# Turning the attention's exponents in 32x32 blocks on VectorE instead of TensorE, from the 12th unit on

## The chip, the cores and the metric

The kernel runs on one core of a Trainium2 chip. The metric is device time in microseconds (us). The kernel before took 911.37 us (median of three runs, 910.83 to 912.17).

## What is computed

A windowed attention over 8 sequences of 576 tokens with 8 heads of 64, whose output feeds a two-layer network with a gate of its own. All of it is in float32.

```python
scores = scale * np.matmul(q, k.transpose(0, 1, 3, 2))          # B, H, S, D = 8, 8, 576, 64
mask_plain = (rel >= 0) & (rel < 32)                            # heads 0-3
mask_dil = (rel >= 0) & (rel < 32 * 4) & (rel % 4 == 0)         # heads 4-7
attn = np.exp(scores - np.max(scores, axis=-1, keepdims=True))
attn = attn / (np.sum(attn, axis=-1, keepdims=True) + 1e-09)
x = np.matmul(attn, v)            # then tokens x 512
h = x @ w_in                      # 4608 x 2048
g = h * erf(softplus(h))
out = g @ w_out                   # 4608 x 512
```

## The kernel before

**Units.** The attention is cut into 72 units of 256 queries for two heads. Dilated heads are reordered on the host, so every strip of 32 queries needs 64 keys. A unit has 8 strips. Its scores lie on 128 partitions (four strips `r` of 32 queries) in two parts `p`, each 64 keys wide, for two heads `h`: 128 x 256 numbers. A unit passes through these steps:

- `scores(n)`, TensorE: 32 matmuls of 32x64 results into the two banks `sp0`, `sp1` (line 221).
- `mask_max(n)`, VectorE: mask and row maximum, four groups of 128x64 (line 232).
- `exponents(n)`, ScalarE: exp and row sums (line 242).
- `normalize(u)`: reciprocal on VectorE (line 254), product on GpSimd (POOL, line 255).
- Three units later, `transposes(u)`, TensorE: two 128x128 transposes against an identity into PSUM (line 260), then `turned(u)`, VectorE: one copy of 128x256 to the tile `pT` (line 264). Now keys lie on partitions.
- `values(u)`, TensorE: 32 matmuls with 64 keys on 64 partitions, with `v` as the weights (line 279).
- `rows(u)`, ScalarE: copies the result out of PSUM (line 321).

**The network.** It works on 512 tokens at a time, in 72 steps `t` of two halves `j`. The loop over `x = 2t + j` gives each engine its work of one half step, in a fixed order written by hand. TensorE's order in one `x` is: the first product (`mm1`, line 528; from the fourth chunk `mm1_fast`, line 649), the second product of two steps earlier (`mm2`, line 702, 12 matmuls of 512 columns), then, if a unit is due, `values` and `scores` (`attend`). VectorE takes the first product out of its single PSUM buffer `h` (and `tx`): `take`, line 670, `take_fast`, lines 658 to 663. It then computes the gate (lines 684 to 688) and, while the weights are being split in two parts, `prep_dve` (lines 460 to 466). ScalarE does softplus and erf (lines 674, 677).

**Visits.** `visits()` tells in which `x` units are scored, and the same `x` turns and multiplies the units scored three units before. The first 14 units (`first_visit`) run before the loop; there units 0 to 10 are turned. Units 11 to 17 are turned singly in `x` = 0 to 6, units 18, 19, 20 singly in `x` = 9, 11, 14, units 21 to 70 in pairs in 25 visits from `x` = 19 to 99, and unit 71 in `x` = 103. For `x` below 4 the turn stands ahead of `mm1`; later it stands between `mm1` and `mm2`:

```python
if t < 2:
    turn(ready)
    weights(x)
...                       # mm1, take
if t >= 2:
    turn(ready)
```

All engines work through their instructions in order. Transfers are issued on one queue (SP), also in order, so a transfer that waits holds up those behind it.

Of the kernel before, what the change touches and what calls it, by code (L numbers as in the profile page):

```python
# [10 lines left out]
F32 = mybir.dt.float32  # L11
# [7 lines left out]
P = 128  # L19
# [45 lines left out]

FREE = FIRST - LAG + 4

EARLY = 2, 3, 4, 6, 7, 9, 10, 12, 13


# [37 lines left out]
def kind(n):  # L108

    it, strip = divmod(n, NSTRIP)  # L110
    at = strip * STRIP
    if it % HP >= HP // 2:

        e = (at + STRIP - 1) // RES * RES - at
        return 1 + EDGES.index(e) if e > -WIN else 0
    return 1 if strip == 0 else 0


def kinds(u, p):

    n = SPU * u + SIDE * p
    return tuple(kind(n + i) for i in range(SIDE))


PARTS = SPU // SIDE
# [4 lines left out]
def key_start(u, s):  # L130

    return s * STRIP + (WIN if (SPU * u) // NSTRIP != (SPU * u + s) // NSTRIP else 0)
# [7 lines left out]
def attn_moe_kernel(ctx: ExitStack, tc: tile.TileContext, qk, v, masks, eye, w_in, w_out, out):  # L140
# [31 lines left out]
        return qkz[u % 3 if u < DEEP else u % 2]  # L172

    vz = [one.tile([P, SIDE, 2, D], F32, name=f"v{i}") for i in range(2)]
    pz = [one.tile([P, n], F32, name=f"pT{i}") for i, n in enumerate((2 * P, TOK))]

    spb = [ps.tile([P, TOK], F32, name=f"sp{i}") for i in range(2)]
    sps = [b[:, 0:2 * PARTS * KEYS].rearrange("p (i b k) -> p i b k", i=2, k=KEYS) for b in spb]
# [35 lines left out]

    def scores(u):
        i, z = u % 2, qk_of(u)
        for s in range(SPU):
            at, (p, r) = QW + key_start(u, s), divmod(s, SIDE)
            for h in range(2):
                hs = slice(h * D, (h + 1) * D)  # L220
                nc.tensor.matmul(sps[h][r * STRIP:(r + 1) * STRIP, i, p, :], z[hs, s * STRIP:(s + 1) * STRIP],  # L221
                                 z[hs, at:at + KEYS], start=True, stop=True,
                                 tile_position=(h * D, r * STRIP))
# [37 lines left out]
                                in_=pr[:, PARTS * h:PARTS * (h + 1), :].rearrange("p a k -> p (a k)"), identity=ident)  # L261

    def turned(u, copy):
        copy(out=pz[u in second][:, 0:2 * P], in_=turn_place(u))

    def turn(units):
        for u in units:
            transposes(u)
        for u in units:
            turned(u, nc.vector.tensor_copy)  # L270

    def values(u):
        vt, pt = vz[u % 2], pz[u in second]
        for s in range(SIDE):
            qs = slice(s * STRIP, (s + 1) * STRIP)
            for p in range(PARTS):
                ks, xp = slice(p * KEYS, (p + 1) * KEYS), place(u, p)
                for h in range(2):
                    nc.tensor.matmul(xp[h * D:(h + 1) * D, qs], vt[ks, s, h, :],  # L279
                                     pt[ks, h * P + s * STRIP:h * P + (s + 1) * STRIP], start=True, stop=True,  # L280
                                     tile_position=(p * KEYS, h * D))
# [432 lines left out]
    def save():  # L714

        o = doubles(2).bitcast(F32).rearrange("p n w -> p (n w)")
        spare = small.tile([P, DM], F32, name="o", bufs=1)
        for tt in range(TOK // P):
            part = [o[:, 0:DM], o[:, DM:2 * DM], spare, pz[1]][tt]
            copy_for(tt)(out=part, in_=acc[tt])  # L720
            nc.sync.dma_start(out=partial[tt], in_=part)

# [21 lines left out]
    with tc.manual_schedule():  # L744
# [26 lines left out]
        for x in range(2 * (NT + 2)):  # L771
# [2 lines left out]
            scored, ready = [n for n in ns if has(n)], [n - LAG for n in ns]  # L774
            second.update(ready[1:])

            if t < 2:
                turn(ready)
                weights(x)
            if t < NT:  # L780
                after = STEPS[t + 1][0] if ends(t) and t + 1 < NT else None
# [22 lines left out]
                table(t - 1)  # L804
            if t < 2:
                attend(ready, scored)
            if t >= 2:
                turn(ready)

            while scaled:  # L810
                normalize(scaled.pop(0))
            scaled, fresh = fresh, []
# [74 lines left out]
def _values(a):  # L887

    p = _padded(a)
    w = np.stack([p[..., i * STRIP:i * STRIP + KEYS, :] for i in range(NSTRIP)], axis=2)  # L890
    w = w.reshape(NU, PARTS, SIDE, 2, KEYS, D).transpose(0, 1, 4, 2, 3, 5)
    return np.ascontiguousarray(w).reshape(NU, PARTS * KEYS, SPU * D)


def _masks():
# [38 lines left out]
```

## Time and profile before

| what | value |
|---|---|
| median of three runs | 911.37 us (910.83 to 912.17) |
| span of the profiled execution, first to last instruction | 908.9 us |
| mean granted TensorE clock | 0.994 |
| TensorE busy | 884.3 us, 97% |
| VectorE busy | 669.6 us, 74% |
| ScalarE busy | 600.7 us, 66% |
| GpSimd busy | 77.9 us, 9% |
| first half step `x` = 0 starts near | 50 us |
| last unit's `values` | 683 us |

The record holds the span of the profiled execution alone; the time outside the span was not recorded with it. The median of the timed runs lies 2.5 us above the span, and sums against the span are carried over to the median by this constant. In the rows of the profile a time is in microseconds from the start of the span; PE is TensorE, DVE VectorE, ACT ScalarE, POOL GpSimd, SPq the queue of transfers; an arrow in brackets names what ended the idle time ahead of an instruction.

### The profile page before, as it was taken

How to read it: one execution, taken by the hardware profiler on the slowest of the kernel's cores; microseconds unless marked ns; L12 is line 12 of the kernel's file. 1: busy time of each engine (PE TensorE's matmuls, PEld its weight loads, DVE VectorE, ACT ScalarE, POOL GpSimd, SP SyncE). 2: the span in 40 equal slices, each digit the busy share in tenths (PEclk: the TensorE clock that was granted, in tenths of full speed). 3: DMA queues.
4: the chain of work that ended last, by engine and by line, in shares of the span. 5: the costliest groups of instructions: out<-in, count | busy, mean ns of one | idle time of the engine just before them, and what ended most of it. 6: DMA issues, size and time to landing. Idle time of an engine off the chain costs nothing.

```text
span 908.9 us, 22857 instructions
## 1 busy us (share of the span) xinstructions
PE 884.3 (97%) x9129; PEld 753.5 (83%) x9129; DVE 669.6 (74%) x1702; ACT 600.7 (66%) x1267; POOL 77.9 (9%) x97
## 2 busy tenths in 40 slices
PE   7789999999999999999999999999999999999998
PEld 3367777888887888889989988888988999999996
DVE  3889879886688888668776777678666866776555
ACT  5889879876678687666776676669654644545442
POOL 2322100000011100000100000000000000000000
PEclk7999999999999999999999999999999999999999
DMA  8784444432458688687668765877567546655521
GB/s 276 250 273 149 137 159 135 136 127 80 150 199 324 232 284 309 241 284 227 219 206 283 262 213 191 289 266 252 185 237 230 185 146 230 233 180 203 199 84 47
DMA packets 69450, 188.89 MB, mean 208 GB/s; under 512 B 9184, under 2 KB 17632, under 8 KB 63200
## 3 DMA queue, kind: packets, MB, share of 16 engines
q1 hardware_dynamic: 69056, 186.91, 60.9%
q8 instruction: 72, 1.18, 0.5%
q10 hardware_dynamic: 288, 0.52, 0.1%
q14 instruction: 34, 0.28, 0.1%
HBM read 153.85 MB, written 33.55 MB: 206 GB/s over the span
## 4 chain that ended last, share of the span: by engine, by line
PE 85%; DVE 7%; DMA 3%; ACT 2%; issue 1%; POOL 1%; SPq 0%; DVEq 0%; POOLq 0%; ACTq 0%
PE acc L702 40%; PE h L649 15%; PE tx L649 12%; PE h L528 10%; PE sp L279 3%; PE sp L221 3%; PE sp L260 1%; DMA dbl<-in_w_in_dram 1%; DMA v<-in_v_dram 1%; DVE s L684 1%; DVE hc L670 1%; DVE w L465 1%; ACT prob L242 1%; DVE prob L232 1%; POOL prob L255 0%
## 5 line engine op out<-in xcount | busy, mean ns | idle before, releaser
L702 PE MATMUL acc<-wout_hi,ghi 128*128 128x512 f32 x576 | 228.4, 397 | 0.5 <-DVE ghi L687 0.4
L702 PE MATMUL acc<-wout_lo,ghi 128*128 128x512 f32 x576 | 225.7, 392 | 0.0
L674 ACT ACTIVATE s<-hc 128x1024 f32<-128x1024 f32 x72 | 76.5, 1062 | 189.4 <-DVE hc L663 171.2
L702 PE MATMUL acc<-wout_hi,glo 128*128 128x512 f32 x576 | 159.0, 389 | 0.0
L702 PEld LDWEIGHTS acc<-wout_hi,glo 128*128 128x128 f32 x576 | 108.1, 188 | 22.7
L702 PEld LDWEIGHTS acc<-wout_hi,ghi 128*128 128x128 f32 x576 | 108.6, 188 | 20.7 <-DVE ghi L687 0.9
L702 PEld LDWEIGHTS acc<-wout_lo,ghi 128*128 128x128 f32 x576 | 108.7, 189 | 19.5
L255 POOL TENSOR_TENSOR prob<-prob,rinv 128x256 f32<-128x256 f32 x72 | 69.0, 968 | 539.0 <-DVE ssum L253 314.1
L688 DVE TENSOR_TENSOR glo<-s,ghi 128x512 fp32r<-128x512 f32 x144 | 100.1, 695 | 5.5 <-PE acc L702 0.5
L242 ACT ACTIVATE prob<-prob,nmax 128x64 f32<-128x64 f32 x288 | 96.4, 338 | 7.6 <-DVE nmax L232 7.1
L684 DVE TENSOR_TENSOR s<-hc,s 128x1024 f32<-128x1024 f32 x72 | 92.9, 1290 | 9.2 <-ACT s L677 9.1
L528 PE MATMUL h<-x,win 128*128 128x512 f32 x384 | 96.6, 394 | 2.6 <-DVE hc L670 2.5
L649 PE MATMUL h<-win 128*128 128x256 f32 x720 | 98.1, 283 | 0.0
L674 ACT ACT_TABLE_LOAD x72 | 92.4, 1283 | 1.3
L677 ACT ACT_TABLE_LOAD x72 | 92.4, 1283 | 1.3
L649 PEld LDWEIGHTS h<-win 128*128 128x128 f32 x720 | 91.6, 192 | 0.0
L528 PEld LDWEIGHTS h<-x,win 128*128 128x128 f32 x384 | 71.2, 188 | 18.8 <-DVE hc L670 3.7
L677 ACT ACTIVATE s<-s 128x1024 f32<-128x1024 f32 x72 | 76.3, 1060 | 0.8
L232 DVE CUSTOM_DVE_ANT_0 prob<-sp,cst 128x64 f32<-128x64 f32 x288 | 45.4, 220 | 36.9 <-ACT rows L321 20.1
L687 DVE CAST ghi<-s 128x512 fp32r<-128x512 f32 x144 | 68.5, 475 | 3.1 <-PE acc L702 0.6
L321 ACT COPY rows<-sp 128x128 f32<-128x128 f32 (+7 forms) x167 | 27.9, 308 | 57.3 <-PE sp L221 55.0
L659 DVE TENSOR_TENSOR hc<-h,hc 128x512 f32<-128x512 f32 x48 | 33.2, 692 | 41.1 <-PE h L649 40.8
(110 smaller groups left out, 1257.6 us busy)
## 6 DMA issues: line engine op xcount, KB each, us to landing
win<-ws SPq DMA_DIRECT2D x48, 1024.0 KB, 5.5
win<-ws SPq DMA_DIRECT2D x48, 768.0 KB, 4.5
v<-in_v_dram SPq DMA_DIRECT2D x72, 256.0 KB, 4.1
qk<-in_qk_dram SPq DMA_DIRECT2D x45, 272.0 KB, 3.9
dbl<-in_w_in_dram SPq DMA_DIRECT2D x16, 512.0 KB, 4.0
dbl<-in_w_out_dram SPq DMA_DIRECT2D x16, 512.0 KB, 3.7
ws<-x SPq DMA_DIRECT2D x32, 256.0 KB, 4.1
xT<-rows SPq DMA_DIRECT2D x24, 288.0 KB, 5.0
```

What stands on the lines that cost most here:

```text
L232: nc.vector.tensor_tensor_reduce(out=pr[:, g, :], in0=sps[h][:, u % 2, p, :], in1=mask[QUADS.index(kinds(u, p))], scale=-SCALE, scalar=BIG ...
L242: nc.scalar.activation(out=probs[u][:, j, :], in_=probs[u][:, j, :], func=AF.Exp, scale=-1.0, bias=nmax[:, j:j + 1], accum_out=sums[u][:, ...
L255: nc.gpsimd.tensor_tensor(probs[u], probs[u], rinv.broadcast_to([P, 2 * PARTS, KEYS]), op=ALU.mult)
L528: nc.tensor.matmul(h, win_at[:, ftp, j, cc // 2, w, cc % 2, :], x[cc], start=(k == 0 and i == 0), stop=(k == CC - 1 and i == 2))
L649: nc.tensor.matmul((h, bank)[b][:, half * HN:(half + 1) * HN], w[:, k, wi, c, :], x[:, xi, c, :], start=(c == 0 and n == 0), stop=(c == 1 ...
L659: nc.vector.tensor_tensor(out=a[:, 0:2], in0=x, in1=a[:, 2:3].broadcast_to([P, 2, HN]), op=ALU.add)
L674: nc.scalar.activation(out=ls[t], in_=hs[t], func=AF.Softplus)
L677: nc.scalar.activation(out=ls[t], in_=ls[t], func=AF.Erf)
L684: nc.vector.tensor_tensor(out=e, in0=hc, in1=e, op=ALU.mult)
L687: nc.vector.tensor_copy(out=ghi, in_=e[:, j])
L688: nc.vector.tensor_tensor(out=glo, in0=e[:, j], in1=ghi.bitcast(F32), op=ALU.subtract)
L702: nc.tensor.matmul(acc[tt], g[:, tt * P:(tt + 1) * P], w[:, ft, :], start=(first and w is wout_hi and g is ghi), stop=(last and g is glo))
```

## The change

From unit 11 (`TURNED = FIRST - LAG`) on, TensorE no longer turns the exponents. VectorE does it from SBUF to SBUF, with an instruction that transposes 32x32 blocks, each within its 32 partitions. One instruction turns the whole 128x256 unit. Half of the blocks are then where `values` can use them; the other half must lie on the neighbouring 32 partitions, and four more instructions of 32 partitions x 128 elements turn these again and write them there. So that 64 keys come to lie on 64 neighbouring partitions, the strips of a unit are dealt to the partitions in another order (`strip_of`), the values and masks are laid out anew on the host, and the masks grow from 10 to 14 groups of 64 columns. `flip` stands at the head of `x`, ahead of `mm1` and `take`, for all later units. `pT` is one tile for both units of a pair, and `save` uses the tile `plain` in place of two others.

```diff
+TURNED = FIRST - LAG
...
 def kinds(u, p):
-    n = SPU * u + SIDE * p
-    return tuple(kind(n + i) for i in range(SIDE))
+    return tuple(kind(SPU * u + strip_of(u, p, r)) for r in range(SIDE))
+
+def strip_of(u, p, r):
+    return SIDE * p + r if u < TURNED else SIDE * (r // 2) + 2 * p + r % 2
...
     def turned(u, copy):
-        copy(out=pz[u in second][:, 0:2 * P], in_=turn_place(u))
-
-    def turn(units):
-        for u in units:
-            transposes(u)
-        for u in units:
-            turned(u, nc.vector.tensor_copy)
+        copy(out=pz[:, 0:2 * P], in_=turn_place(u))
+
+    def flip(units):
+        for i, u in enumerate(units):
+            to = pz[:, i * 2 * P:(i + 1) * 2 * P].rearrange("p (e g q) -> p e g q", e=2, q=STRIP)
+            src = probs.pop(u).rearrange("p g (e k) -> p e g k", e=2)
+            nc.vector.transpose(out=to.rearrange("p e g q -> p g e q"), in_=src.rearrange("p e g k -> p g e k"))
+            for r in range(SIDE):
+                y, q = r % 2, r ^ 1
+                nc.vector.transpose(out=to[q * STRIP:(q + 1) * STRIP, y], in_=src[r * STRIP:(r + 1) * STRIP, 1 - y])
...
     def values(u):
-        vt, pt = vz[u % 2], pz[u in second]
+        if u >= TURNED:
+            vt, at = vz[u % 2].rearrange("p (y a) h d -> p y a h d", y=2), (u in second) * 2 * P
+            for y in range(2):
+                for p in range(PARTS):
+                    for x in range(2):
+                        ks = slice(x * KEYS, (x + 1) * KEYS)
+                        qs = slice((2 * p + y) * STRIP, (2 * p + y + 1) * STRIP)
+                        for h in range(2):
+                            c = at + y * P + (PARTS * h + p) * STRIP
+                            nc.tensor.matmul(place(u, x)[h * D:(h + 1) * D, qs], vt[ks, y, p, h, :],
+                                             pz[ks, c:c + STRIP], start=True, stop=True,
+                                             tile_position=(x * KEYS, h * D))
+            return
...
     def save():
-        spare = small.tile([P, DM], F32, name="o", bufs=1)
-            part = [o[:, 0:DM], o[:, DM:2 * DM], spare, pz[1]][tt]
+            part = [o[:, 0:DM], o[:, DM:2 * DM], plain[:, TOK:2 * TOK], plain[:, 0:TOK]][tt]
...
+            flip(ready)
             if t < 2:
-                turn(ready)
                 weights(x)
...
-            if t >= 2:
-                turn(ready)
```

VectorE in `x` = 1, where unit 12 is turned: the masks of unit 14 end, then the turn, the weights, a remainder of the attention's result and `take`. Before:

```order
L232 ISA nmax 128x1
L264 COPY pT_88<-acc_94 128x256
L460 TENSOR_TENSOR win<-w,win 128x4x128
L464 TENSOR_SCALAR w<-w 128x512
L465 SCALAR_TENSOR_TENSOR w<-dbl_891,w 128x512
L466 SCALAR_TENSOR_TENSOR w<-dbl_891,w 128x512
L332 TENSOR_TENSOR wout_lo<-rows,wout_hi 128x448
L670 COPY hc<-h 128x512
```

After the change, in the same place:

```order
L239 ISA nmax 128x1
L278 STREAM_TRANSPOSE pT<-prob 128x4x2x32
L281 STREAM_TRANSPOSE pT<-prob 32x128 x4
L484 TENSOR_TENSOR win<-w,win 128x4x128
L488 TENSOR_SCALAR w<-w 128x512
L489 SCALAR_TENSOR_TENSOR w<-dbl_890,w 128x512
L490 SCALAR_TENSOR_TENSOR w<-dbl_890,w 128x512
L356 TENSOR_TENSOR wout_lo<-rows,wout_hi 128x448
L694 COPY hc<-h 128x512
```

Five instructions stand where one copy stood; nothing else moved here.

VectorE in `x` = 59, a visit of a pair (units 45 and 46). `w` at line 615 belongs to the next chunk, lines 662 and 663 are `take_fast`, 684 to 688 the gate. Before:

```order
L615 TENSOR_TENSOR w<-dbl_5166,x_97 128x512
L615 TENSOR_TENSOR w<-dbl_5167,dbl_5166 128x512
L662 TENSOR_TENSOR hc<-tx,hc 128x2x256
L663 TENSOR_TENSOR hc<-h,hc 128x512
L264 COPY pT_88<-sp_90 128x256
L264 COPY pT_89<-sp_91 128x256
L684 TENSOR_TENSOR s<-hc,s 128x1024
L687 CAST ghi<-s 128x512
L688 TENSOR_TENSOR glo<-s,ghi 128x512
```

After the change:

```order
L639 TENSOR_TENSOR w<-dbl_5232,x_96 128x512
L639 TENSOR_TENSOR w<-dbl_5233,dbl_5232 128x512
L278 STREAM_TRANSPOSE pT<-prob 128x4x2x32
L281 STREAM_TRANSPOSE pT<-prob 32x128 x4
L278 STREAM_TRANSPOSE pT<-prob 128x4x2x32
L281 STREAM_TRANSPOSE pT<-prob 32x128 x4
L686 TENSOR_TENSOR hc<-tx,hc 128x2x256
L687 TENSOR_TENSOR hc<-h,hc 128x512
L708 TENSOR_TENSOR s<-hc,s 128x1024
L711 CAST ghi<-s 128x512
L712 TENSOR_TENSOR glo<-s,ghi 128x512
```

The turn has moved from behind `take_fast` to ahead of it, and has ten instructions in place of two.

TensorE in the same visit, between `mm1_fast` and `mm2`, before:

```order
L649 MATMUL h<-win 128x256 x12
L260 MATMUL sp_90<-ident,prob 128x128 x2
L260 MATMUL sp_91<-ident,prob 128x128 x2
L702 MATMUL acc_93<-wout_hi,ghi 128x512
L702 MATMUL acc_93<-wout_lo,ghi 128x512
```

After the change the two rows of line 260 are gone and `mm2` follows `mm1_fast` at once; the rest of TensorE's list is the same, matmul by matmul, and so are ScalarE's, POOL's and the queue of transfers, but for the names of tiles and the wider transfer of the masks.

More of the change, by code (lines that the diff above doesn't have):

```diff
@@ L174, in attn_moe_kernel @@
     vz = [one.tile([P, SIDE, 2, D], F32, name=f"v{i}") for i in range(2)]
-    pz = [one.tile([P, n], F32, name=f"pT{i}") for i, n in enumerate((2 * P, TOK))]
+    pz = one.tile([P, TOK], F32, name="pT")
     spb = [ps.tile([P, TOK], F32, name=f"sp{i}") for i in range(2)]
@@ L216, in scores @@
         i, z = u % 2, qk_of(u)
-        for s in range(SPU):
-            at, (p, r) = QW + key_start(u, s), divmod(s, SIDE)
+        for p, r in np.ndindex(PARTS, SIDE):
+            s = strip_of(u, p, r)
+            at = QW + key_start(u, s)
             for h in range(2):
@@ L263, in turned @@
     def turned(u, copy):
-        copy(out=pz[u in second][:, 0:2 * P], in_=turn_place(u))
-    def turn(units):
-        for u in units:
-            transposes(u)
-        for u in units:
-            turned(u, nc.vector.tensor_copy)
-    def values(u):
-        vt, pt = vz[u % 2], pz[u in second]
+        copy(out=pz[:, 0:2 * P], in_=turn_place(u))
[7 more added lines that the diff above has]
+                nc.vector.transpose(out=to[q * STRIP:(q + 1) * STRIP, y], in_=src[r * STRIP:(r + 1) * STRIP, 1 - y])
+    def values(u):
+        if u >= TURNED:
[11 more added lines that the diff above has]
+            return
+        vt, pt = vz[u % 2], pz
         for s in range(SIDE):
@@ L890, in _values @@
     w = np.stack([p[..., i * STRIP:i * STRIP + KEYS, :] for i in range(NSTRIP)], axis=2)
-    w = w.reshape(NU, PARTS, SIDE, 2, KEYS, D).transpose(0, 1, 4, 2, 3, 5)
-    return np.ascontiguousarray(w).reshape(NU, PARTS * KEYS, SPU * D)
+    w = w.reshape(NU, SPU, 2, KEYS, D)
+    units = []
+    for u in range(NU):
+        if u < TURNED:
+            units.append(w[u].reshape(PARTS, SIDE, 2, KEYS, D).transpose(0, 3, 1, 2, 4))
+        else:
+            units.append(w[u].reshape(2, PARTS, 2, 2, KEYS, D).transpose(0, 4, 2, 1, 3, 5))
+    return np.stack([x.reshape(PARTS * KEYS, SPU * D) for x in units])
 def _masks():
```

## The prediction, made before the kernel was run

> **What bounds the kernel now.** I read the page first (busy shares), then the busy times by stage, then the two engines' timelines at the turns, then the waits. The profiled execution's span is 908.9 us; the median of the runs lies 2.5 us higher, and I add that at the end.
>
> ```profile
> span 908.9 us, 22857 instructions
> PE 884.3 (97%) x9129; PEld 753.5 (83%) x9129; DVE 669.6 (74%) x1702; ACT 600.7 (66%) x1267; POOL 77.9 (9%) x97
> ```
>
> TensorE is the bound on the average, and VectorE has a quarter of the span free. The average hides the stages:
>
> ```profile
> 54.00:75.00 21.00, 17.22 (x277) 12.85 (x255) 18.94 (x66) 18.93 (x46) 4.01 (x7) 1.00 0.82 278
> 75.00:97.00 22.00, 22.00 (x276) 17.29 (x275) 18.06 (x57) 19.69 (x57) 2.61 (x4) 1.00 0.44 136
> 97.00:143.00 46.00, 44.31 (x371) 34.98 (x370) 39.80 (x85) 36.53 (x67) 5.93 (x5) 1.00 0.41 133
> 143.00:245.00 102.00, 102.00 (x919) 84.05 (x921) 78.25 (x186) 76.63 (x142) 7.92 (x7) 1.00 0.39 127
> 245.00:300.00 55.00, 53.98 (x695) 43.70 (x692) 46.70 (x148) 41.62 (x113) 8.10 (x8) 1.00 0.72 250
> 300.00:350.00 50.00, 48.83 (x426) 39.46 (x424) 44.18 (x109) 36.54 (x75) 3.35 (x4) 1.00 0.77 269
> 350.00:684.00 334.00, 334.00 (x3913) 299.80 (x3907) 242.85 (x657) 223.78 (x495) 29.35 (x30) 1.00 0.71 243
> ```
>
> Behind the limits of a stage (us from the span's start) stand its length and the busy times of TensorE, of its weight loads, of VectorE, ScalarE and POOL, each with its count of instructions. From 143 to 245 and from 350 to 684 TensorE never rests, and VectorE is idle for 24 and 91 us. In 54 to 143, 245 to 300 and 300 to 350 VectorE is idle for only 12.2, 8.3 and 5.8 us, and TensorE itself waits there. The change takes work from TensorE and gives more of it to VectorE, so each stage has to be settled by itself.
>
> **What TensorE saves.** A half step without a turn and one with a pair's turn:
>
> ```profile
> 404.95 1.60 PE L649 MATMUL h<-win 128*128 128x256 f32 x12
> 406.39 0.40 PE L702 MATMUL acc<-wout_hi,ghi 128*128 128x512 f32 x1
> 406.63 0.40 PE L702 MATMUL acc<-wout_lo,ghi 128*128 128x512 f32 x1
> ...
> 415.47 1.60 PE L649 MATMUL h<-win 128*128 128x256 f32 x12
> 416.91 0.60 PE L260 MATMUL sp<-ident,prob 128*128 128x128 f32 x4
> 417.27 0.48 PE L702 MATMUL acc<-wout_hi,ghi 128*128 128x512 f32 x1
> 417.58 0.39 PE L702 MATMUL acc<-wout_lo,ghi 128*128 128x512 f32 x1
> ```
>
> From the start of the 12 matmuls to the second of `mm2` it is 1.68 us without and 2.11 us with the four transposes: 0.43 us for a pair, 0.215 us for a unit. For 61 units that is 13.1 us, if nothing takes its place. The Trainium skill (TensorE: Matmul & The Clock Gate, Part 4: PE-mode transpose) has about 275 ns for a 128x128 transpose inside a kernel; by it 122 transposes are worth an estimated 34 us. The duration of one agrees here, but they overlap, so the saving is that of the distances.
>
> `values` and `scores` keep their number, shapes and order of array positions: no change. The masks (10 to 14 groups) make one transfer 40% longer; it is hidden behind the wait for the first scores, and I put 0 to 0.3 us, taken as 0. `save` copies and stores as much as before: 0.
>
> **What VectorE pays.** No row shows a 32x32 transpose. Nearest are the copy of 128x256, the mask's 128x64, and two dependent operations of 128x256:
>
> ```profile
> 55.73 0.22 DVE L232 CUSTOM_DVE_ANT_0 prob<-sp,cst 128x64 f32<-128x64 f32 x1
> 55.88 0.22 DVE L232 CUSTOM_DVE_ANT_0 prob<-sp,cst 128x64 f32<-128x64 f32 x1
> ...
> 417.72 0.75 DVE L264 COPY pT<-sp 128x256 f32<-128x256 f32 x2
> L264 DVE COPY pT<-sp x57: 408/415/425, 74.6 to 680.8; 128x256 f32<-128x256 f32 x57
> ...
> 250.06 0.42 DVE L547 TENSOR_TENSOR plain<-plain 128x256 f32<-128x256 f32 x1
> 250.51 0.42 DVE L548 TENSOR_TENSOR plain<-plain 128x256 f32<-128x256 f32 x1
> ```
>
> From start to start it is 0.15 us for 64 columns. Two copies of 0.42 us (median 415 ns) take 0.75 together, so the second starts 0.33 after the first; a line through 64 and 256 columns gives 0.21 for 128. Where the next one needs the result it is 0.45 for 256. The first small transpose overwrites blocks of the large one and waits for it; the other three wait for nothing. One unit: 0.45 + 4 x 0.21 = 1.29 us, less the copy's 0.33: **0.96 us more**, 59 us over 61 units. Bounds: if narrow ones go as fast as 64 columns, 0.33 + 4 x 0.15 = 0.93; if none overlaps, 0.45 + 4 x 0.29 (half way from 0.22 to 0.42, since 128 columns lie between) = 1.6. I take 1.29, since the copy of the same 128x256 is the nearest row and it overlaps.
>
> **Stage by stage.** *54 to 143, ten single turns.* Here the waits are VectorE's:
>
> ```profile
> 55.67 3.02 PE L528 MATMUL h<-x,win 128*128 128x512 f32 x12 [1.13 <-DVE hc L670]
> 64.70 0.67 PE L279 MATMUL acc<-pT,v 64*64 64x32 f32 x32 [1.50 <-DMA v<-in_v_dram]
> 70.56 3.02 PE L528 MATMUL h<-x,win 128*128 128x512 f32 x12 [0.70 <-DVE hc L670]
> ...
> 81.08 0.69 DVE L670 COPY hc<-h 128x512 f32<-128x512 f32 x1 [1.38 <-PE h L528]
> 94.93 0.69 DVE L670 COPY hc<-h 128x512 f32<-128x512 f32 x1 [1.68 <-PE h L528]
> 118.61 0.69 DVE L670 COPY hc<-h 128x512 f32<-128x512 f32 x1 [1.11 <-PE h L528]
> 131.45 0.69 DVE L670 COPY hc<-h 128x512 f32<-128x512 f32 x1 [0.65 <-PE h L528]
> 135.71 1.23 DVE L684 TENSOR_TENSOR s<-hc,s 128x1024 f32<-128x1024 f32 x1 [3.21 <-ACT s L677]
> ```
>
> In the first four half steps the turn stands on the chain masks, turn, weights, `take`, next `mm1`. Ten turns add 9.6 us. The turn of unit 16 follows its normalization at once and waits about 0.8 us for POOL, with `take` queued behind it. Against these 10.4 us stand VectorE's waits ahead of `take` (1.38, 1.68, 1.11, 0.65) and the wait for `v` (1.50), whose transfer is issued behind a weight transfer that waits for VectorE and so slips by the first turn alone: 6.3 us. The wait of 3.21 is no cover: its end hangs on a transfer that can only start once `save` has copied, which is VectorE's work. That leaves 4.1 us of lag, of which TensorE feels some 0.7 less, since `take` has that much room while `mm2` runs: **+3.4 us**. The 2.2 us of transposes that TensorE saves here are not counted, since it would wait for VectorE in their place.
>
> *143 to 245, four pairs.* Each pair adds 1.9 us to VectorE, with 6 us idle for each: fully covered, **-1.7 us**. *245 to 300, four pairs, two half steps apart.* 8 x 0.96 = 7.7 us meet 8.3 idle, while TensorE's own work falls by 1.7 us and by its waits for POOL (1.0):
>
> ```profile
> PE sp L260 <- POOL prob L255: 1.0, 3, 0.7
> 281.29 0.61 POOL L255 TENSOR_TENSOR prob<-prob,rinv 128x256 f32<-128x256 f32 x1 [10.73 <-DVE rinv L254]
> ```
>
> VectorE then needs 46.7 + 7.7 = 54.4 of the 55 us and is the bound; I leave it about 0.9 us of waits that no turn can fill, and the gain is gone: **+0.3**. The late unit's product (0.61 us) is hidden behind the turn of the earlier one. *300 to 350, two pairs.* The end is set by VectorE:
>
> ```profile
> 348.22 0.68 DVE L670 COPY hc<-h 128x512 f32<-128x512 f32 x1
> 349.29 1.45 PE L279 MATMUL sp<-pT,v 64*64 64x32 f32 x64 [0.49 <-DVE pT L264]
> ```
>
> With the turns ahead of line 670 the first unit is ready at 348.22 + 1.29 = 349.5, the second at 350.8; `values` of the second waits until then and all that follows ends 0.7 us later. For the pair near 321 I take 0, between -0.4 (its transposes saved) and +1.9 (its turns in full), since 5.8 us of idle stand against the stage's 3.8. **+0.7.** *350 to 684, fifteen pairs and one unit.*
>
> ```profile
> 415.67 0.69 DVE L662 TENSOR_TENSOR hc<-tx,hc 128x512 f32<-128x512 f32 x1
> 417.11 0.69 DVE L663 TENSOR_TENSOR hc<-h,hc 128x512 f32<-128x512 f32 x1 [0.75 <-PE h L649]
> 420.19 1.14 PE L279 MATMUL sp<-pT,v 64*64 64x32 f32 x64
> 422.05 1.69 PE L649 MATMUL tx<-win 128*128 128x256 f32 x12
> ACT s L674 <- DVE hc L663: 171.2, 33, 5.8
> ```
>
> The turns take the place ahead of line 662, from 415.6 to 418.2; `values` needs them at 420.19 - 0.43 = 419.8. Lines 662 and 663 follow and end at 419.5 in place of 417.8, and the next matmuls into their buffers start at 422.05 - 0.43 = 421.6. Softplus (line 674), queued behind it on ScalarE, slips 1.7 us, and ScalarE waits 5 us a time there. All is covered: 15 x 0.43 + 0.2 = **-6.7 us**.
>
> Sum: 3.4 - 1.7 + 0.3 + 0.7 - 6.7 = -4.0 us; 904.9 for the span, **907.4 us** for the median.
>
> **The rivals.** *Dear transposes (slower).* Some 21 turns (10 + 8 + 3) lie where VectorE sets the pace, so each 0.1 us more for a turn costs 2.1 us, and at 1.48 us a turn the gain is gone. If none overlaps (1.6) the result is +2.5: 913.9. If each column takes twice as long, a turn is about 2.0 us and the result +11: 922. For it speaks that no row shows the operation and that four of five write to other partitions than they read; against it, that every plain VectorE row here overlaps with the next. The Trainium skill (VectorE: DVE Perf Modes, The three transpose paths) has 311 ns for a 128x128 transpose on VectorE. Taken as the distance of the small ones it makes a turn an estimated 1.69 us and the time about 916; as a duration, which the profile here shows to overlap, it agrees with 0.29 within a tenth.
>
> *Lag that costs nothing (faster still).* If VectorE's lag before 143 is met by slack that I don't see, or a turn costs 0.93 us, the 21 turns give back up to 7.5 us: 900 to 904. All 13.1 us and the 1.0 of POOL waits would be 897; the rows of 54 to 143 speak against it.
>
> *A wash.* Waits for the turn in the close visits (two half steps apart) after 350, or ScalarE slipping with `take`, eat 2 to 6 us: 909.5 to 913. VectorE's idle of 91 us against 30 turns is against it, the crowded 245 to 350 for it.
>
> **Chances.** Forecast (904 to 909.5) 0.50, faster still 0.13, a wash 0.17, dear transposes 0.20. A measurement of this kernel can tell about 0.2% (1.8 us) from no change. Faster by over 0.2%: 0.63; within it: 0.17; slower: 0.20. The range, 901 to 917, leaves out the far ends of the two outer cases.
>
> **What will show it.** Small transposes 0.21 us apart and 1.29 us from the first to `take`; no line for 128x128 transposes after unit 10; `mm2` right behind `mm1`, so that visits after 350 are 0.43 us shorter (fifteen of them: the last `values` about 4 us earlier than 683); new TensorE waits for line 670's successor before 143, about 3 us in sum. I am wrong if small transposes stand 0.3 us apart or more, or if TensorE waits for `pT` after 350.

## The result, and the profile after

The changed kernel took 921.54 us (median of four runs, 920.65 to 923.17), against 911.1 us before. The ratio is 1.0122, with a 95% interval of 1.0102 to 1.0141: slower by 10.4 us, where 4.0 us less had been forecast, and outside the range of 901 to 917. One execution of experiment 12 took 3295 us; its ratio leaves it out. The head of the page of the profiled execution:

```profile
span 919.4 us, 22806 instructions
PE 886.9 (96%) x9007; PEld 749.0 (81%) x9007; DVE 745.1 (81%) x1946; ACT 599.2 (65%) x1267; POOL 83.3 (9%) x97
PE 65%; DVE 23%; DMA 4%; issue 3%; ACT 3%; SPq 1%; POOL 0%; DVEq 0%; POOLq 0%; ACTq 0%
```

VectorE is busy for 75.5 us more, where 59 had been reckoned, and its share of the chain that ended last (third line) has grown from 7 to 23%. The turn itself, from the groups by tile and from VectorE's timeline in the visit of units 45 and 46:

```profile
L281 DVE STREAM_TRANSPOSE pT<-prob x244: 299/304/308, 53.3 to 689.6; 32x128 f32<-32x128 f32 x122
L278 DVE STREAM_TRANSPOSE pT<-prob x61: 414/439/447, 52.9 to 688.1; 128x256 f32<-128x256 f32 x61
427.78 0.43 DVE L278 STREAM_TRANSPOSE pT<-prob 128x256 f32<-128x256 f32 x1
428.25 1.29 DVE L281 STREAM_TRANSPOSE pT<-prob 32x128 f32<-32x128 f32 x4
429.57 0.45 DVE L278 STREAM_TRANSPOSE pT<-prob 128x256 f32<-128x256 f32 x1
```

A small transpose lasts 304 ns. Four of them fill 1.29 us, so they start (1.29 - 0.304) / 3 = 0.33 us apart, further than they last: none of the four overlaps the next. From the start of one turn to the start of the next it is **1.79 us**, where the forecast had 1.29.

What TensorE then waits for, in the changed kernel (in all, times, longest; us):

```profile
PE h L552 <- DVE hc L694: 9.6, 8, 2.5
PE tx L673 <- DVE hc L684: 2.9, 3, 1.3
PE sp L293 <- DVE pT L281: 2.8, 8, 0.4
PE acc L726 <- DVE dbl L743: 2.2, 1, 2.2
```

The first row stood at 2.5 us, 3 times, before the change. Line 694 is `take`, line 743 the copy of `save`, and line 281 the small transposes, which `values` now waits for piece by piece. The places of the two longest waits, the second unit of a pair, whose `values` wait twice, and a wait of `take_fast`:

```profile
75.61 5.49 PE L552 MATMUL h<-x,win 128*128 128x512 f32 x12 [2.52 <-DVE hc L694]
135.14 0.50 PE L726 MATMUL acc<-wout_hi,ghi 128*128 128x512 f32 x1 [2.17 <-DVE dbl L743]
308.15 0.30 PE L293 MATMUL sp<-pT,v 64*64 64x32 f32 x4 [0.39 <-DVE pT L281]
308.80 0.76 PE L293 MATMUL sp<-pT,v 64*64 64x32 f32 x28 [0.34 <-DVE pT L281]
453.66 0.98 PE L673 MATMUL tx<-win 128*128 128x256 f32 x6 [1.33 <-DVE hc L684]
```

The busy times by stage, in the columns of the prediction:

```profile
54.00:75.00 21.00, 15.40 (x296) 11.37 (x294) 19.94 (x66) 15.71 (x42) 1.59 (x3) 0.92 0.72 237
75.00:97.00 22.00, 21.39 (x198) 16.95 (x199) 19.54 (x62) 17.78 (x52) 4.90 (x7) 0.84 0.32 107
245.00:300.00 55.00, 53.02 (x704) 42.17 (x703) 52.87 (x161) 38.76 (x99) 6.08 (x6) 1.00 0.58 202
350.00:684.00 334.00, 328.18 (x3813) 291.60 (x3812) 287.78 (x795) 226.13 (x497) 33.38 (x30) 1.00 0.71 244
```

VectorE has 2.1 us left of 55 in the third row. The granted clock, third from the end, was 1.00 in the first two rows before the change.

To see where the time went, I mark the starts of `values` of some units, which are the same work in all kernels. For the changed kernel (the row of unit 10 carries the other line of `values`, 303):

```profile
50.61 0.88 PE L303 MATMUL acc<-pT,v 64*64 64x32 f32 x32
150.79 0.30 PE L293 MATMUL sp<-pT,v 64*64 64x32 f32 x4
251.53 1.14 PE L293 MATMUL sp<-pT,v 64*64 64x32 f32 x64
307.05 0.70 PE L293 MATMUL sp<-pT,v 64*64 64x32 f32 x32
385.83 1.14 PE L293 MATMUL sp<-pT,v 64*64 64x32 f32 x64
693.56 0.67 PE L293 MATMUL sp<-pT,v 64*64 64x32 f32 x32
```

The same marks of the other kernels give the lengths between them (us; the last column is the fifth experiment, below). The differences are taken before rounding. The stretches end at visits: units 41 and 42 are turned after 350 us, so their 0.43 us is moved here from the forecast's last term, -6.7, to the one before it, +0.7:

| stretch between `values` of | before | after | difference | forecast | turn of 1.29 us |
|---|---|---|---|---|---|
| start to unit 10 (nothing turned by VectorE) | 49.0 | 50.6 | +1.6 | 0 | 51.1 |
| unit 10 to unit 20 (ten single turns) | 92.5 | 100.2 | +7.7 | +3.4 | 95.9 |
| unit 20 to units 27, 28 (four pairs) | 102.0 | 100.7 | -1.2 | -1.7 | 100.5 |
| to units 35, 36 (four close pairs) | 55.4 | 55.5 | +0.1 | +0.3 | 53.7 |
| to units 41, 42 (three pairs) | 74.2 | 78.8 | +4.5 | +0.3 | 77.1 |
| to unit 71 (fifteen visits) | 309.9 | 307.7 | -2.2 | -6.2 | 303.5 |

The first row is no effect of a turn: over the fourteen kernels, alike up to there but for the masks, unit 10 begins between 46.1 and 51.1 us, and the granted clock goes with it. From 10 to 50 us that was 0.96 in the six traces where unit 10 begins before 48 us, 0.86 to 0.87 in three (48.3 to 49.2; the kernel before is one) and 0.74 to 0.77 in five (from 49.5 on; the changed kernel is one). From unit 10 to unit 71 the changed kernel takes 8.9 us more; whether the medians of the timed runs hold a share of the other 1.6 is not on record.

### The profile page after: what moved, and what is told of

Same layout as the page of the kernel before. It is cut to its first block, busy times and chain, and to the rows that moved or that the text cites. A ratio compares the mean times of both kernels' runs of the same rounds, so it can differ in the third digit from the quotient of the medians.

```text
span 919.4 us, 22806 instructions
## 1 busy us (share of the span) xinstructions
PE 886.9 (96%) x9007; PEld 749.0 (81%) x9007; DVE 745.1 (81%) x1946; ACT 599.2 (65%) x1267; POOL 83.3 (9%) x97
## 4 chain that ended last, share of the span: by engine, by line
PE 65%; DVE 23%; DMA 4%; issue 3%; ACT 3%; SPq 1%; POOL 0%; DVEq 0%; POOLq 0%; ACTq 0%
PE acc L726 31%; PE h L673 13%; PE tx L673 10%; PE h L552 6%; DVE pT L281 4%; DVE s L708 2%; PE sp L293 2%; PE sp L228 2%; DMA dbl<-in_w_in_dram 2%; DVE prob L239 1%; DVE pT L278 1%; DVE hc L694 1%; DVE ghi L711 1%; DVE w L489 1%; DVE glo L712 1%
## 5 line engine op out<-in xcount | busy, mean ns | idle before, releaser
L262 POOL TENSOR_TENSOR prob<-prob,rinv 128x256 f32<-128x256 f32 x72 | 73.7, 1033 | 545.9 <-DVE ssum L260 303.8
L712 DVE TENSOR_TENSOR glo<-s,ghi 128x512 fp32r<-128x512 f32 x144 | 103.5, 719 | 5.5 <-PE acc L726 0.5
L552 PE MATMUL h<-x,win 128*128 128x512 f32 x384 | 100.8, 406 | 6.9 <-DVE hc L694 6.9
L552 PEld LDWEIGHTS h<-x,win 128*128 128x128 f32 x384 | 74.1, 195 | 24.4 <-DVE hc L694 7.9
L708 DVE TENSOR_TENSOR s<-hc,s 128x1024 f32<-128x1024 f32 x72 | 87.9, 1221 | 4.5 <-ACT s L701 4.1
L281 DVE STREAM_TRANSPOSE pT<-prob 32x128 f32<-32x128 f32 x244 | 73.9, 303 | 6.7
L673 PE MATMUL tx<-win 128*128 128x256 f32 x432 | 60.5, 285 | 2.7 <-DVE hc L684 2.7
L673 PEld LDWEIGHTS tx<-win 128*128 128x128 f32 x432 | 57.1, 190 | 7.2 <-DVE hc L684 3.5
```

The source lines that it names most:

```text
L262: nc.gpsimd.tensor_tensor(probs[u], probs[u], rinv.broadcast_to([P, 2 * PARTS, KEYS]), op=ALU.mult)
L281: nc.vector.transpose(out=to[q * STRIP:(q + 1) * STRIP, y], in_=src[r * STRIP:(r + 1) * STRIP, 1 - y])
L552: nc.tensor.matmul(h, win_at[:, ftp, j, cc // 2, w, cc % 2, :], x[cc], start=(k == 0 and i == 0), stop=(k == CC - 1 and i == 2))
L673: nc.tensor.matmul((h, bank)[b][:, half * HN:(half + 1) * HN], w[:, k, wi, c, :], x[:, xi, c, :], start=(c == 0 and n == 0), stop=(c == 1 ...
L708: nc.vector.tensor_tensor(out=e, in0=hc, in1=e, op=ALU.mult)
L712: nc.vector.tensor_tensor(out=glo, in0=e[:, j], in1=ghi.bitcast(F32), op=ALU.subtract)
```

## The experiments

The theory was *price*: the change does what was forecast, but a turn costs 1.79 us and VectorE sets the pace in the crowded stages. Its rivals were *place* (the turn ahead of `take` is what hurts) and *clock* (TensorE's lower granted clock before 140 us).

**1. Without the small transposes.**

```diff
             nc.vector.transpose(out=to.rearrange("p e g q -> p g e q"), in_=src.rearrange("p e g k -> p g e k"))
-            for r in range(SIDE):
-                ...
```

> Leaves out the four small transposes of every turn, so half of the turned blocks are not the reference's; all else is as in the changed kernel. A turn then holds VectorE for 0.47 us in place of 1.79, about 0.14 more than the copy it replaced. Theory 'price' (the small transposes do not overlap, so a turn costs 1.79 us and VectorE sets the pace in the crowded stages): TensorE's saving comes through nearly whole, 13 us less about 1.5 us for ten turns before 143: 899 to 902 us. Rival 'place' (the turn ahead of take is what hurts, whatever it costs): VectorE still works ahead of take in every visit, TensorE's waits before 143 and around 360 stay, 910 us or more.

Measured: 900.16 us, ratio 0.9867 (0.9839 to 0.9894). The turn stands at the same place and the kernel is 21 us faster than the changed one: the place alone does not hurt. A turn costs less than was expected, since the next large transpose does not wait for the one ahead; VectorE's timeline at units 45 and 46:

```profile
410.93 0.44 DVE L278 STREAM_TRANSPOSE pT<-prob 128x256 f32<-128x256 f32 x1
411.29 0.40 DVE L278 STREAM_TRANSPOSE pT<-prob 128x256 f32<-128x256 f32 x1
```

The second starts 0.36 after the first, which lasts 0.44: a large transpose overlaps as a copy does, and a turn is 0.36. From units 41, 42 to unit 71 it takes 303.5 us, 6.4 less than before, where TensorE was to save 6.2.

**2. Pairs only.** Units 11 to 20 go back to TensorE:

```diff
+def flipped(u):
+    return u >= 21
...
-            flip(ready)
+            fl, tu = [u for u in ready if flipped(u)], [u for u in ready if not flipped(u)]
+            flip(fl)
             if t < 2:
+                turn(tu)
                 weights(x)
...
+            if t >= 2:
+                turn(tu)
```

> TensorE turns units 11 to 20 as before the change (transposes and copy, at their old places); VectorE turns units 21 to 71 as in the changed kernel. By the stages of the two traces the first ten turns cost 9.8 us up to 143 us. Theory 'price': this loss goes and nothing else changes, 911 to 913 us, no different from before. Rival 'clock' (the lower granted clock in the first 140 us, 0.84 to 0.96, is a state of the run and not a consequence of the turns): the clock stays low there and the time is 916 us or more.

Measured: 913.37 us, ratio 1.0018 (1.0004 to 1.0033), and a granted clock of 1.00 from 54 to 97 us. The loss before 143 us is gone, and the low clock with it. TensorE's wait for the copy of `save` is back at 0.2 us, as before the change, though the new `save` stands; so the 2.2 us did not come from its new place. The pairs in sum gain nothing and rather lose a little.

**3. Filling TensorE's gaps.**

```diff
             if t < 2:
                 attend(ready, scored)
+                warm(8)
```

> The changed kernel with 8 more bf16 matmuls of 512 columns (results unused, into the bank that is not in use yet) at the end of each of the first four half steps, where TensorE waits up to 2.5 us for VectorE. Theory 'clock follows the gaps': with the gaps filled the granted clock stays at 1.00 from 54 to 97 us, the 12 matmuls of line 552 near 76 us take 3.0 us in place of 5.5, and the time falls by 2 to 5 us, to 917 to 919. Theory 'price alone': VectorE sets the pace there whatever TensorE's clock is, the time falls by less than 1.5 us, 920 to 922.

Measured: 918.33 us, ratio 1.0080 (1.0055 to 1.0106). TensorE's timeline shows the clock's part:

```profile
72.52 3.02 PE L557 MATMUL h<-x,win 128*128 128x512 f32 x12 [0.50 <-DVE hc L699]
54.00:75.00 21.00, 19.89 (x264) 13.32 (x264) 19.97 (x66) 17.77 (x40) 3.31 (x6) 1.00 0.75 250
```

The 12 matmuls take 3.02 us in place of 5.49 and the clock stays at 1.00, as *clock follows the gaps* has it. But the stretch from unit 10 to unit 20 is still 99.4 us, against 100.2 in the changed kernel and 92.5 before: with TensorE at full clock VectorE sets the same pace. The two profiled runs differ by 3.7 us already ahead of unit 10, where their programs are alike (46.9 against 50.6 us), so I don't count the 3.2 us between the medians as the filling's. The intervals of the two ratios touch.

**4. What makes the small ones dear.** Every third unit keeps them, every third transposes in place, every third copies:

```diff
+                if u % 3 == 0:
+                    nc.vector.transpose(out=to[r * STRIP:(r + 1) * STRIP, y], in_=src[r * STRIP:(r + 1) * STRIP, 1 - y])
+                elif u % 3 == 1:
+                    nc.vector.tensor_copy(out=to[q * STRIP:(q + 1) * STRIP, y], in_=src[r * STRIP:(r + 1) * STRIP, 1 - y])
...
```

> Measures the disputed operation. In every third unit the four small operations stay as they are; in every third they are transposes that write to their own 32 partitions; in every third plain copies that write to the neighbouring 32 partitions (so two thirds of the units are not the reference's). Theory 'transpose': both transposes take 0.30 us and stand 0.33 apart, the copy 0.2 to 0.29 and stands about 0.2 apart. Theory 'neighbour': the transpose in place stands about 0.21 apart, and both that write to the neighbour 0.33.

Measured, in VectorE's groups (busy time, mean ns of one) and its timeline; line 286 is the original, 282 in place, 284 the copy:

```profile
L286 DVE STREAM_TRANSPOSE pT<-prob 32x128 f32<-32x128 f32 x84 | 25.4, 303 | 2.3
L282 DVE STREAM_TRANSPOSE pT<-prob 32x128 f32<-32x128 f32 x80 | 24.2, 303 | 2.2
L284 DVE COPY pT<-prob 32x128 f32<-32x128 f32 x80 | 17.8, 222 | 2.2
241.28 1.29 DVE L282 STREAM_TRANSPOSE pT<-prob 32x128 f32<-32x128 f32 x4
243.08 0.95 DVE L284 COPY pT<-prob 32x128 f32<-32x128 f32 x4
```

In place or to the neighbour, a small transpose lasts 303 ns, and four fill 1.29 us. So the write to other partitions is not what is dear. Four copies to the neighbour fill 0.95 and start (0.95 - 0.222) / 3 = 0.24 apart: each is 0.08 shorter, but they don't overlap either. The missing overlap is thus no property of the transpose; experiments 11 and 12 look for what it belongs to. The one run took 915.97 us.

**5. The price of the forecast.** One transpose, two copies, the fourth operation left out:

```diff
-            for r in range(SIDE):
+            for r in range(SIDE - 1):
+                if r == 0: nc.vector.transpose(...)
+                else:      nc.vector.tensor_copy(...)
```

> Gives a turn the price of the forecast: of the four small operations one stays a transpose (0.33 us), two become plain copies of the same blocks (0.24 each by the last run) and the fourth is left out, so a turn holds VectorE for 0.47 + 0.33 + 0.49 = 1.29 us in place of 1.79; the output is not the reference's. Theory 'only the price was wrong': the forecast's sum holds, 906 to 909 us. Rival 'the stages were read too kindly as well': the ten turns before 143 and the pairs from 300 to 373 cost more than the 3.4 and 0.7 us of the forecast even at this price, 910 to 915 us.

Measured: **907.39 us**, ratio 0.9946 (0.9925 to 0.9968), against the forecast's 907.4 (0.9956 of 911.4). The turn was what it was meant to be, from 420.19 to 421.48:

```profile
420.19 0.44 DVE L278 STREAM_TRANSPOSE pT<-prob 128x256 f32<-128x256 f32 x1
420.67 0.30 DVE L282 STREAM_TRANSPOSE pT<-prob 32x128 f32<-32x128 f32 x1
421.00 0.45 DVE L284 COPY pT<-prob 32x128 f32<-32x128 f32 x2
421.48 0.45 DVE L278 STREAM_TRANSPOSE pT<-prob 128x256 f32<-128x256 f32 x1
```

At this price the change pays. That the median falls on the forecast to the tenth is luck: the five runs spread from 904.5 to 909.4, the profiled one being the slowest. Stage by stage the sum was less exact than its total: the last column of the table has -1.7 where +0.3 had been reckoned (to units 35, 36) and +2.8 where +0.3 had (to units 41, 42), two errors that nearly cancel; the other terms are within 0.3 us. From unit 10 to unit 71 it is -3.4, where the terms of the forecast add up to -4.0.

**6. VectorE turns only where it has room.** Of this edit and of those of experiments 7 and 9 only the choice of units is shown; the rest is that of experiment 2.

```diff
+def flipped(u):
+    return 21 <= u < 29 or u >= 41
```

> VectorE turns only the pairs of the stages in which it has room (units 21 to 28 and 41 to 71, in 143 to 245 and from 350 on); TensorE turns all others as before the change. Theory 'price, by stage': 143 to 245 gives -1.6 us as in the changed kernel, 245 to 350 is as before the change, and from 350 on about -2.3 (fifteen pairs at -0.45 and one unit, less three waits after close visits, 1.3, 0.3 and 1.3): 907 to 909 us. Rival 'mixing': leaving the crowded stage to TensorE frees nothing, since the lag there comes from the stage's own work: the time stays at 911 to 914, that of the kernel with all pairs turned by VectorE.

Measured: 906.67 us, ratio 0.9946 (0.9926 to 0.9967). This version beats both kernels by its median, and its interval lies below 1. Between units 27, 28 and 41, 42 it takes 129.2 us, as against 129.7 before and 134.3 after. From there to unit 71 it is 307.7 us, the same as in the changed kernel, with the same waits for `take_fast`:

```profile
PE tx L684 <- DVE hc L695: 2.9, 3, 1.3
```

**7. Only the ten single turns.**

```diff
+def flipped(u):
+    return FIRST - LAG <= u < 21
```

> VectorE turns only units 11 to 20, the ten single turns before 143 us; TensorE turns all later ones as before the change. Theory 'the early turns are most of the loss': 9.8 us by the marks of the two traces, 919 to 922 us, as slow as the changed kernel, and with the 2 us of the run that had only the pairs the two parts add up to its 10.4. Rival 'the parts hide each other': a lag before 143 is worked off in the roomy stage behind it when nothing is turned there, under 916.

Measured: 921.1 us, ratio 1.0111 (1.0089 to 1.0134). Ten turns of 61 lose what all of them lose together, and nothing is worked off later. Unit 20 starts at 150.9 us, as in the changed kernel. With experiment 2 (+2) the parts add up to 11.6, against 10.4.

**8. The turn behind `take`.**

```diff
-            flip(ready)
             if t < 2:
+                flip(ready)
...
+            if t >= 2:
+                flip(ready)
```

> The changed kernel with the turn behind take from the third step on, where the copy stood before, in place of ahead of it; nothing else differs. Theory 'price' (VectorE's work is what counts, and its place decides only who waits): take is earlier, but the second unit of a pair is turned about 4.3 us after mm1 ends while its values are due after 2.75, so TensorE waits 1 to 1.5 us in each of 25 visits: 935 to 960 us. Rival 'place' (the turn ahead of take is what hurts): the time falls below 918.

Measured: 946.48 us, ratio 1.0385 (1.0368 to 1.0401). `values` now waits for the turn in nearly every visit:

```profile
PE sp L293 <- DVE pT L281: 13.5, 38, 0.7
```

At 1.79 us a turn the old place is worse by 25 us; the place that the change chose helped it.

**9. Leaving out close visits too.**

```diff
+def flipped(u):
+    return 21 <= u < 27 or u >= 41 and u not in (47, 48, 51, 52, 65, 66, 69, 70)
```

> As the kernel in which VectorE turns only in the roomy stages, but the pairs next to another visit two half steps away (units 27 and 28, and the second visit of each of the three close couples after 350 us: units 47, 48, 51, 52, 65, 66, 69, 70; where a couple's lag reaches the next visit the first one's neighbour is taken) are left to TensorE as well. Theory 'price, by visit': the two waits of 1.3 us for the take after close visits go, and four or five pairs' savings of 0.45 us are given up: 0.5 to 1 us less than the kernel before it, 905 to 906.5. Rival: those waits are a part of the visits' normal overlap and come back elsewhere; the lost savings remain, 908 to 909.

Measured: 907.37 us, ratio 0.9958 (0.9943 to 0.9974), not to be told from experiment 6. The waits for `take_fast` fell from 2.9 to 0.3 us, but the stretch from units 41, 42 to unit 71 is 307.9 us, no shorter. Its waits from 364 us on show one reason:

```profile
PE sp L271 <- POOL prob L266: 1.1, 2, 0.6
PE tx L684 <- DVE hc L695: 0.3, 1, 0.3
```

In two of the four close visits that TensorE now turns, it waits for POOL's product, which follows a normalization that stands behind VectorE's late work. With four pairs' savings given up (1.7 us) that leaves the stretch where it was. The time lies between the two expectations; that the stretch got no shorter is what the rival said.

**10. The price of the forecast with the gaps filled.** The edits of experiments 3 and 5 together.

> The kernel with a turn of 1.29 us (one small transpose, two copies, the fourth operation left out) together with the 8 filling matmuls at the end of each of the first four half steps. From the values of unit 10 to those of unit 20 the kernel before takes 92.5 us, the changed kernel 100.2, the filled one 95.5 and the one with a turn of 1.29 us 95.9. Theory 'the early reckoning was right': VectorE's lag of 3.4 us is there with any clock, the stretch stays at 95 to 96.5 us and the time at 906 to 908. Rival 'right by luck': part of the 3.4 us was the lower clock, which the forecast had not reckoned with; the stretch falls to 92.5 to 94.5 us and the time to 904 to 906.

Measured: 904.87 us, where the kernel before took 909.53 in the same runs; ratio 0.9945 (0.9927 to 0.9963), the same as without filling. The stretch from unit 10 to unit 20 is 94.6 us, between the two expectations: +2.1 us over before at full clock, +3.4 without the filling. Some 1.3 us of the early term may have been the clock, the rest was VectorE's lag. But the five kernels in which TensorE makes these ten turns take 91.3 to 93.0 us for this stretch, so 1.3 is within what one trace differs from another, and the total does not show a difference.

**11. What prevents the overlap.** Two transposes in place of four, whose partitions vary from unit to unit:

```diff
+            for y in range(2):
+                if u % 3 == 0:
+                    nc.vector.transpose(out=to[:, y], in_=src[:, 1 - y])
+                elif u % 3 == 1:
+                    nc.vector.transpose(out=to[0:STRIP, y], in_=src[0:STRIP, 1 - y])
+                else:
+                    nc.vector.transpose(out=to[y * 2 * STRIP:(y + 1) * 2 * STRIP, y], in_=src[...])
...
```

> Behind the large transpose stand, in place of the four small ones, two that depend on nothing but it: for every third unit two of all 128 partitions by 128 columns, for every third two on the same first 32 partitions, for every third one on the lower and one on the upper 64 partitions. The blocks that the small ones would bring to the neighbouring partitions are left out. Three theories for the missing overlap. Kind (no transpose overlaps): the second starts 0.30 us or more after the first in all three, two fill 0.60 to 0.64. Against it stands that in the run without small transposes two large ones of 0.437 filled 0.77, so started 0.33 apart. Width (an instruction on fewer than 128 partitions does not overlap): the two of 128 partitions start 0.20 to 0.25 apart and fill 0.50 to 0.56, the others 0.33 apart and fill 0.63. Quadrant (the change of partitions from one to the next): those on the same 32 partitions fill 0.50 to 0.56 as well, and only the two halves of 64 fill 0.63. The length of one is 0.30 in all, if it goes by columns. The time, by 3.2 us for each 0.1 us of a turn: a turn is 0.47 + 0.55 to 0.63 = 1.0 to 1.1 us, under the forecast's 1.29, so 903 to 906 us.

Measured, in VectorE's groups and its timeline; line 281 is on all 128 partitions, 283 on the first 32, 285 on the lower and then the upper 64:

```profile
L285 DVE STREAM_TRANSPOSE pT<-prob 64x128 f32<-64x128 f32 x42 | 12.9, 306 | 1.4
L281 DVE STREAM_TRANSPOSE pT<-prob 128x128 f32<-128x128 f32 x40 | 10.1, 291 | 0.7
L283 DVE STREAM_TRANSPOSE pT<-prob 32x128 f32<-32x128 f32 x40 | 9.8, 278 | 0.7
391.18 0.30 DVE L283 STREAM_TRANSPOSE pT<-prob 32x128 f32<-32x128 f32 x1
391.42 0.26 DVE L283 STREAM_TRANSPOSE pT<-prob 32x128 f32<-32x128 f32 x1
391.61 0.39 DVE L278 STREAM_TRANSPOSE pT<-prob 128x256 f32<-128x256 f32 x1
392.03 0.64 DVE L285 STREAM_TRANSPOSE pT<-prob 64x128 f32<-64x128 f32 x2
392.71 0.69 DVE L691 TENSOR_TENSOR hc<-tx,hc 128x512 f32<-128x512 f32 x1
415.47 0.51 DVE L281 STREAM_TRANSPOSE pT<-prob 128x128 f32<-128x128 f32 x2
416.33 0.49 DVE L283 STREAM_TRANSPOSE pT<-prob 32x128 f32<-32x128 f32 x2
416.76 0.64 DVE L691 TENSOR_TENSOR hc<-tx,hc 128x512 f32<-128x512 f32 x1
```

*Quadrant* holds. Of two on the same 32 partitions the second starts 0.24 after the first (391.18, 391.42), before that one's end, and lasts 0.26 in place of 0.30; two on all 128 partitions fill 0.51 and are as far apart. Two on different halves fill 0.64 and are 0.33 apart. The neighbours sharpen it: the large one behind those on the first 32 partitions starts (391.61) before they end (391.67), though it is four times as wide. Line 691, the same instruction in both visits, starts after the end (392.67) of the upper half (392.71), but before the end (416.82) of a pair on the first 32 partitions (416.76). Width does not matter; what goes with the overlap is that both begin at the same partition. The four small ones of the change begin, each of them, at another partition than the one ahead. The one run took 904.33 us, as expected.

**12. Two units side by side.** Experiment 6, with the small transposes of a pair's units in turn:

```diff
             nc.vector.transpose(out=to.rearrange("p e g q -> p g e q"), in_=src.rearrange("p e g k -> p g e k"))
-            for r in range(SIDE):
-                y, q = r % 2, r ^ 1
+            turns.append((to, src))
+        for r in range(SIDE):
+            y, q = r % 2, r ^ 1
+            for to, src in turns:
                 nc.vector.transpose(out=to[q * STRIP:(q + 1) * STRIP, y], in_=src[r * STRIP:(r + 1) * STRIP, 1 - y])
```

> As the sixth run, but the two units of a pair are turned side by side: both large transposes first, then each small one of the earlier unit with its like of the later unit behind it, on the same 32 partitions. By quadrant (only an instruction on other partitions than the one ahead waits for that one's end) the large ones start 0.33 apart, the first small one 0.47 after the second large one, and the eight small ones alternate between 0.21 and 0.33: 0.33 + 0.47 + 4 x 0.21 + 4 x 0.33 = 2.96 us for a pair from its start to the next instruction, against 3.58, so 1.48 a unit. The kernel then gains over the sixth run what lies between 1.79 and 1.29 us a turn in the close visits from unit 41 on (307.7 against 303.5 us), by 0.31 of 0.50: 2.6 us, 904 us. Rival, waiting: the earlier unit's small ones now stand behind the later unit's large one, which waits for POOL's product in the visits where that comes late; VectorE loses up to 0.6 us there and the time stays at 906 to 907 us, though the pair itself takes 2.96 where nothing waits. If quadrant is wrong, the small ones stay 0.33 apart and a pair takes 3.44.

Measured: 905.01 us, ratio 0.9949 (0.9932 to 0.9965). VectorE's timeline in two visits:

```profile
412.02 0.76 DVE L290 STREAM_TRANSPOSE pT<-prob 128x256 f32<-128x256 f32 x2
412.82 2.03 DVE L295 STREAM_TRANSPOSE pT<-prob 32x128 f32<-32x128 f32 x8
414.87 0.69 DVE L700 TENSOR_TENSOR hc<-tx,hc 128x512 f32<-128x512 f32 x1
...
426.12 0.45 DVE L290 STREAM_TRANSPOSE pT<-prob 128x256 f32<-128x256 f32 x1 [0.49 <-POOL prob L266]
```

The pair takes 2.85 us from 412.02 to 414.87, where it took 3.59 in experiment 6: the order of the same ten instructions is worth 0.74 us. The 2.85 is less than the 2.96 expected, since an overlapped small transpose is also shorter (0.26): the eight start 0.24 and 0.27 apart in turn, where 0.21 and 0.33 had been put. The time does not show it. From units 41, 42 to unit 71 it is 306.4 us, 1.3 less than in experiment 6, of the 2.6 expected; the ratio can't be told from 0.9946. In some visits, as in the second one shown, VectorE now waits for POOL's product of the later unit (1.9 us in 4 waits), which the earlier unit's small transposes used to hide. Both theories had a part in it.

## Why the prediction was wrong

- **The step that failed is the price of a turn.** The prediction took 0.45 + 4 x 0.21 = 1.29 us, "since the copy of the same 128x256 is the nearest row and it overlaps". Measured are 0.47 + 4 x 0.33 = 1.79. Every VectorE row that had been read for the overlap was of 128 partitions; "the other three wait for nothing" overlooked that each of the four begins at another partition than the one ahead, and there 0.33 is the distance. The 0.21 was also a little small: transposes that begin at the same partition are 0.24 apart (experiment 11). So of the 0.50 us by which a turn is dearer, about 0.37 is the missing overlap, 0.1 the size of the distance and 0.02 the large transpose. Copies that change partitions do not overlap either (experiment 4), so the missing overlap is not one of the transpose alone.
- **The bound failed too.** The upper one, 1.6, let durations add up without overlap, but took 0.29 for one and no gap, where it is 0.304 and a gap of 0.03.
- **Both named signs of being wrong came.** The small transposes stand 0.33 apart, and TensorE waits for `pT` after 350 us, three times and 1.1 us in all, near 362.
- **The rival was named, with a chance of 0.20.** It was *dear transposes*, 913.9 to 922, and 921.5 came. Its case "if none overlaps" is what happened, but for that it had 913.9; that the measured time lies near its upper end, which stood for another cause (each column twice as long), is luck. The Trainium skill (VectorE: DVE Perf Modes, The three transpose paths) has 311 ns for a 128x128 transpose in bf16. As a duration, as the prediction read it, it agrees with experiment 11 (291 ns for 128x128 in float32, and the next one starts 0.24 after it). Read as a distance it gave an estimated 1.69 us a turn and 916 us, nearer to what came, for a reason that has nothing to do with it.
- **The sum held at its own price** (experiment 5: -3.4 for -4.0, with two errors of 2 us and more that nearly cancel). TensorE's saving was sized well: from unit 20 to units 27, 28 -1.2 for -1.7 and, with cheap turns, -6.4 for -6.2 behind units 41, 42.
- **The slope was too flat at the dear end.** The prediction had 2.1 us for each 0.1 us of a turn and a break-even at 1.48. The kernels with turns of 0.36, 1.29 and 1.79 us stand at ratios of 0.9867, 0.9946 and 1.0122 to before: 0.8 us per 0.1 below the forecast's price, 3.2 above it. A straight line between the last two puts the break-even at 1.44. With 2.1 the dear price would have given 917.9.
- **The early term**: +7.7 in place of +3.4. By experiments 3 and 10 it is VectorE's pace; the lower clock is a consequence of TensorE's gaps and had little of its own to add. The clock was not in the reckoning at all.
- **From 350 us on**: -2.2 in place of -6.2. "All is covered" failed, in four visits of fifteen. The other eleven come after the visit ahead of them 0.42 to 0.45 us sooner than before (the last one 0.21), as forecast. The visits of units 49, 50 and 67, 68, behind two of the four couples of visits that stand two half steps apart, come 1.2 us later than before: there two pairs' turns of 1.79 us delay `take_fast`, and TensorE waits 1.33 us. Those of units 57, 58 and 59, 60 lose what they should gain; one wait of 0.29 us shows there, and the rest has no single wait that I can name. Of the rivals, *a wash* comes nearest to this: it had waits in the close visits.
- **300 to 373 us**: +4.5 in place of +0.3, and +2.8 even at the forecast's price, so this term was too kind. What shows from 300 us on is `values` waiting piece by piece for the small transposes (2.4 us, 7 times), `take` 0.5 us more than before, and 0.8 us in which TensorE waits for nothing that the profile shows. That this is the whole of it is not shown, nor that the price is: with turns of 0.36 us (experiment 1) the stretch still took 77.9 us, 3.8 of it in one wait for nothing that the profile shows. Leaving these units to TensorE removes the loss (experiment 6).
- **Not settled**: why another first partition prevents the overlap, and whether the one read or the one written decides (in the change both vary each time). In experiment 12 the first small one (412.82) reads from the same partitions on as the large one ahead and writes to others, and it starts after that one's end (412.78); that speaks for the written one, but whether it waited for a result is not shown.

## What to carry to other kernels

When work moves to an engine that is free on the average, settle it stage by stage, and find the price at which the gain is gone before trusting a price that no row shows: here 0.15 us a turn stood between a gain and none. A price taken from another kind of instruction needs as upper bound its full duration and a gap, since overlap can depend on what stands ahead: here on whether both begin at the same partition. So the order of small instructions on parts of the partitions has a price of its own. And a moved job can be moved in part: left where the receiving engine has idle time, the same turn gains 0.5%.

## What the runs showed of the hardware

- On VectorE an instruction that begins at another partition than the one ahead started only after that one's end (small transposes 0.304 long and 0.33 apart, copies 0.222 and 0.24), while independent ones that begin at the same partition overlapped by 0.06 to 0.08 (transposes 0.24 apart for 128 columns, 0.36 for 256, and copies of 256 0.33), whether they cover 32 or 128 partitions.
- The time of a transpose goes by its columns, not its partitions: 128 columns took 278 to 306 ns on the average on 32, 64 and 128 partitions, 256 columns 427 to 439.
- A transpose of 32 partitions to the neighbouring 32 costs what one in place costs (303 ns both).
- After TensorE's wait of 2.5 us the same 12 matmuls took 5.49 us in place of 3.02, with a granted clock of 0.84 in that stage; filled with idle matmuls, the clock stayed at 1.00.
